# One-batch units first in a block-sparse attention and ELU feed-forward kernel: another order of loading, staging and buffering

## The chip, the cores and the metric

The kernel runs on one core of one Trainium2 chip. The metric is the device time of one execution in microseconds (us), the median of the runs. The core's engines are TensorE (PE; its weight loads are PEld), VectorE (DVE), ScalarE (ACT), GpSimd (POOL) and SyncE (SP), which issues most of the transfers.

## The reference

Attention over four batches of eight heads, 768 positions of width 64, in blocks of 32. A block of queries sees its neighbours, the first and the last block, and three sampled blocks; the first and the last block see everything. The attended rows, 3072 of width 512, then pass a feed-forward layer with an ELU. The weights arrive as 64-bit floats.

```python
scores = scale * np.matmul(q, k.transpose(0, 1, 3, 2))
mask = np.abs(blk_i - blk_j) <= window
mask = mask | (blk_i == 0) | (blk_j == 0) | (blk_i == n_blocks - 1) | (blk_j == n_blocks - 1)
for qb in range(n_blocks):
    for kb in sampled_blocks[qb]:
        mask[qb * block:(qb + 1) * block, kb * block:(kb + 1) * block] = True
attn = softmax(np.where(mask, scores, -1000000000.0))     # over the keys
x = np.matmul(attn, v)                  # rows in the order batch, position, head
h = x @ w_in                            # 3072 x 512 times 512 x 2048
g = np.where(h > 0.0, h, np.exp(np.minimum(h, 0.0)) - 1.0)
return g @ w_out                        # 3072 x 2048 times 2048 x 512
```

## The kernel before

Every operand of a matmul is held as a high and a low f16 part, and products are made of two or three such parts.

**Units.** The batches go in two pairs. A pair has 12 units of 128 query rows (four blocks of 32). `of_one` makes a unit of four blocks of one batch, `of_two` of two blocks of each batch of the pair; one special unit per pair holds the first and the last blocks. `ALONE` says how many one-batch units each batch has: 1 before, so units 0 and 1 lie in batch 0 and batch 1 alone, and from unit 2 on every unit needs the keys and values of both batches. Two units make one tile of the feed-forward layer, so there are 12 tiles; I call them tile 0 to tile 11.

**A unit** (`attention`): its queries are loaded (L640), split into high and low and turned (on PE against an identity for units below `NPE`, L385 and L680, otherwise by a transposing transfer, L377). The sampled values come into a room of `VT` by 12 band transfers or fewer (L726 to L728) and indirect gathers of GpSimd (L733); the sampled keys are copied into `kG` by GpSimd (L748, L755). Then for each of four head pairs: scores on PE (L786), their maximum on DVE (L797), the exponential on ACT (L815) into `e`, its high and low part into `p` (L299 or L297, and L820), a turn of `p` into `pT`, the product with the values on PE (L835), a sum on DVE (L844). `e` and `p` have two rooms each. At the end the rows are normalised (L852 to L854), split and turned into `xT`.

**A tile** (`ffn`): eight steps. A step has two `h` groups of 12 matmuls (L883), ACT and DVE work for the ELU (L893, L895, L891), a split into `g` (L299 or L297, and L900), and, later, two `o` groups of 6 matmuls (L906), one for each half of the tile's rows.

**Preparation.** Keys of batches 0 and 1 are loaded (L511), split (L301, L497), turned on PE and copied into `kT[0]` and `kT[1]`. Values are split and written out to a table in device memory, `vd` (L569), from which the units read them. The weights come in 32 pieces of 512 KB (L429, L433) into rooms that are free at that time (`wo_room`, later two rooms of the tag `st4`); each piece takes two passes of ACT (L439, L444), two of DVE (L451, L455), a cast and a subtraction (L462), which leave the high and the low part in `wi` and `wo`.

**What sets the order.** Each operation has a priority, the engines that may run it with a duration, and the buffers it reads and writes. `Plan.order` walks through a model of the core in time and fixes, ahead of the run, which engine runs what and in which order. On the chip each engine then goes through its list in that order; an instruction that has to wait holds back all behind it on its engine. Priorities are set at L921 to L950: the weights start at `WI`, `WID` apart; a tile at `F0 + T * U`; its units `LEAD` earlier; the second batch's keys and values at `SECOND`.

## Time and profile before

| what | value |
|---|---|
| median of 3 runs | 768.09 us (767.81 to 771.01) |
| profiled execution, first to last instruction | 780.8 us |
| PE busy | 703.2 us (90%) |
| DVE busy | 504.7 us (65%) |
| ACT busy | 406.1 us (52%) |
| POOL busy | 398.8 us (51%) |
| moved by transfers | 126.34 MB, mean 162 GB/s |
| mean granted TensorE clock | 0.934 of full speed |

A busy share is that of the whole span, so it averages a head in which the inputs and weights are prepared and a long stretch in which PE runs without a break. The profiled execution is one of its own, and 1.7% longer than the median run. Tables over stretches show which engine is full where.

### The profile page before, as it was taken

What the parts mean: (1) busy time and instruction counts of PE and PEld (TensorE: products, weight loads), DVE (VectorE), ACT (ScalarE), POOL (GpSimd) and SP (SyncE); (2) the same over time, 40 slices, a digit from 0 to 9 for tenths busy, and PEclk for the clock granted to TensorE, in tenths of its full rate; (3) what the DMA queues carried; (4) which work ended last, traced back from release to release, by engine and by line L of the source; (5) the groups of instructions that cost most, each with busy time, mean ns of one, the idle gap of its engine ahead of it and who ended that gap; (6) DMA issues with size and microseconds to landing.
All of it is one profiled execution on the core that took longest, in us unless ns stands there. A gap on an engine that the chain in (4) does not pass through costs nothing.

```text
span 780.8 us, 26302 instructions
## 1 busy us (share of the span) xinstructions
PE 703.2 (90%) x11064; PEld 476.2 (61%) x11064; DVE 504.7 (65%) x849; ACT 406.1 (52%) x723; POOL 398.8 (51%) x605
## 2 busy tenths in 40 slices
PE   6445466999999998999999999999999999999997
PEld 3334355666665765666866766657656667676663
DVE  7788778898866772767677665757555546644121
ACT  4597767897753743535575443425414344342221
POOL 2588567677553345554375454645625337443121
PEclk7555569999999999999999999999999999999999
DMA  9899998889749697769947987987349459652101
GB/s 240 263 275 288 261 257 209 215 158 208 154 91 264 187 192 164 161 133 203 221 87 142 171 149 150 183 144 166 76 94 229 69 103 216 141 97 45 38 1 27
DMA packets 217006, 126.34 MB, mean 162 GB/s; under 512 B 173944, under 2 KB 194552, under 8 KB 216888
## 3 DMA queue, kind: packets, MB, share of 16 engines
q1 hardware_dynamic: 211608, 107.09, 64.8%
q0 software_dynamic: 5280, 17.58, 8.9%
q8 instruction: 86, 1.41, 0.8%
q14 instruction: 32, 0.26, 0.1%
HBM read 82.05 MB, written 13.21 MB: 122 GB/s over the span
## 4 chain that ended last, share of the span: by engine, by line
PE 80%; issue 4%; DMA 4%; DVE 4%; ACT 3%; POOL 3%; POOLq 1%; SPq 1%; another core or an unknown queue 1%; ACTq 0%; DVEq 0%
PE o L906 32%; PE h L883 31%; PE s L786 6%; PE w L835 4%; PE av L835 2%; PE s L385 2%; DMA wo<-in_moe_w_out_dram 2%; ACT e L815 1%; PE av L385 1%; POOLq L751 1%; DMA VT<-vd 1%; POOL kG L755 1%; DMA raw<-in_sampled_blocks_dram 1%; POOL kG L748 1%
## 5 line engine op out<-in xcount | busy, mean ns | idle before, releaser
L883 PE MATMUL h<-xT,wi 128*128 128x256 f16 x2304 | 281.6, 275 | 4.7 <-DVE fe L891 4.0
L906 PE MATMUL o<-wo,g 128*128 128x512 f16 x1152 | 274.9, 381 | 0.9 <-issue 0.6
L883 PEld LDWEIGHTS <-wi 128*128 128x128 f16 x2304 | 220.0, 98 | 53.8 <-issue 7.1
L906 PEld LDWEIGHTS <-g 128*128 128x128 f16 x1152 | 107.0, 98 | 111.2 <-issue 4.2
L900 POOL TENSOR_TENSOR g<-fe,g 128x512 f16<-128x512 f32 x75 | 90.0, 1200 | 150.8 <-DVE g L299 134.8
L820 POOL TENSOR_TENSOR p<-e,p 128x512 f16<-128x512 f32 x94 | 113.1, 1206 | 93.8 <-DVE p L299 46.4
L893 ACT ACTIVATE fe<-h 128x512 f32<-128x512 f32 x96 | 57.3, 596 | 178.0 <-PE h L883 165.1
L891 DVE SCALAR_TENSOR_TENSOR fe<-h,fe 128x512 f32<-128x512 f32 x96 | 66.0, 688 | 92.9 <-ACT fe L895 84.4
L815 ACT ACTIVATE e<-s,m 128x256 f32<-128x256 f32 x208 | 86.2, 470 | 74.7 <-POOL p L820 37.1
L755 POOL COPY kG<-kT 128x128 int32 x264 | 78.5, 341 | 44.9 <-PE s L786 25.9
L797 DVE TENSOR_REDUCE m<-s 128x2 f32<-128x512 f32 x104 | 70.1, 686 | 44.4 <-PE s L786 41.4
L733 POOL DMA_INDIRECT VT<-vd,idx x66 | 64.5, 977 | 25.1 <-issue 10.1
L895 ACT ACTIVATE fe<-fe,gs 128x512 f32<-128x512 f32 x96 | 69.4, 723 | 2.4
L844 DVE TENSOR_REDUCE x<-w 128x130 f32<-128x260 f32 x64 | 27.2, 426 | 59.7 <-PE w L835 56.9
L835 PEld LDWEIGHTS <-pT 128*32 128x32 f16 x3456 | 43.2, 97 | 36.1 <-issue 33.7
L786 PE MATMUL s<-kG,qT 128*32 128x160 f16 x704 | 44.8, 247 | 9.6 <-ACT e L815 7.0
L786 PEld LDWEIGHTS <-qT 128*32 128x32 f16 x1664 | 33.2, 99 | 31.8 <-issue 26.7
L786 PE MATMUL s<-kT,qT 128*32 128x96 f16 (+1 forms) x832 | 48.5, 225 | 1.2 <-issue 1.0
L786 PE MATMUL s<-kT,qS 128*32 128x96 f16 (+1 forms) x832 | 48.3, 225 | 0.5 <-issue 0.5
L786 PE MATMUL s<-kG,qS 128*32 128x160 f16 x704 | 44.2, 246 | 4.1 <-DVE qS L299 2.7
L299 DVE CAST p<-e 128x512 f16<-128x512 f32 x59 | 32.0, 546 | 13.3 <-DMA pT<-p 6.1
L786 PEld LDWEIGHTS <-qS 128*32 128x32 f16 x1664 | 34.5, 102 | 6.0 <-DVE qS L299 3.0
(134 smaller groups left out, 812.5 us busy)
## 6 DMA issues: line engine op xcount, KB each, us to landing
VT<-vd SPq DMA_DIRECT2D x44, 195.0 KB
VT<-vd SPq DMA_DIRECT2D x22, 390.0 KB
wo<-in_moe_w_out_dram SPq DMA_DIRECT2D x12, 512.0 KB
st<-in_q_dram SPq DMA_DIRECT2D x40, 128.0 KB
out_dram<-ro SPq DMA_DIRECT2D x38, 128.0 KB
wo<-in_moe_w_in_dram SPq DMA_DIRECT2D x9, 512.0 KB
st<-in_moe_w_in_dram SPq DMA_DIRECT2D x7, 512.0 KB
VT<-vd SPq DMA_DIRECT2D x12, 260.0 KB
```

The costliest lines, as they stand in the source:

```text
L733: nc.gpsimd.indirect_dma_start(VT[0:96, 2 * vt.slot, xs[0] : xs[-1] + 1].rearrange("p b x -> p (b x)"), None, d.ap, bass.IndirectOffsetOnA ...
L755: nc.gpsimd.tensor_copy(dst[:, :, r * 16 : (r + 1) * 16], src[:, :, bass.ds(at[r], 16)])
L786: nc.tensor.matmul(dst, lhsT=qq.ap[:, h, j * BLK : (j + 1) * BLK], rhs=mv, start=first, stop=(y == 1 and qq is qS and o0 + w == 256))
L797: nc.vector.tensor_reduce(m.ap[:, 2 * c : 2 * c + 2] if sp else m.ap[:, 6:8], ss[c].ap, axis=AX.X, op=ALU.max, negate=True)
L815: nc.scalar.activation(e32.ap[:, y, :], ss[c].ap[:, y, :], AF.Exp, bias=m.ap[:, 6 + y : 7 + y])
L820: plan.add(LO, t + PITCH * hp + 1, margin=MO, fn=lambda e, e32=e32, p=p: ENG[e].tensor_tensor(p.ap[:, 1, :], flat(e32.ap), p.ap[:, 0, :], ...
L835: nc.tensor.matmul(av.ap[j * BLK : (j + 1) * BLK, y, v0:], lhsT=pts[c].ap[:, pl * 4 + y * 2 + z, j * BLK : (j + 1) * BLK], rhs=VT[:, room, ...
L883: nc.tensor.matmul(h.ap[:, a, :], lhsT=w[:, wl, cs], rhs=x.ap[:, xl, cc, :], start=(n == 0), stop=(n == 3 * NCC - 1))
L891: nc.vector.scalar_tensor_tensor(e32.ap, h.ap, -IH * GS, e32.ap, op0=ALU.mult, op1=ALU.min)
L895: plan.add({"ACT": 0.68}, p0 + 2.6, lambda e, e32=e32: nc.scalar.activation(e32.ap, e32.ap, AF.Relu, bias=gs_col, scale=-GS), r=[e32], w=[ ...
L900: plan.add(LO, p0 + 2.6, margin=MO, fn=lambda e, e32=e32, g=g: ENG[e].tensor_tensor(g.ap[:, 1], e32.ap, g.ap[:, 0], op=ALU.subtract), r=[e ...
L906: nc.tensor.matmul(o.ap, lhsT=g.ap[:, gl, f % 2, m * P : (m + 1) * P], rhs=wo[f][:, wl, :], start=(f == 0 and n == 0), stop=(f == NFC - 1 ...
```

## The change

- `ALONE` goes from 1 to 5. Units 0 to 4 now lie in batch 0 alone, units 5 to 9 in batch 1, the special unit is unit 10, and unit 11 is the one unit of two batches. The second pair of batches keeps its units.
- Only batch 0's keys and values are prepared ahead of the weights, values first. Batch 1's keys and values go through the general `keys` and `values`, at `SECOND` = 36 instead of -110; `values` can now make one batch alone.
- While `kT[1]` is empty its 12 KB per partition are three more rooms for weight pieces (`kt_room`). The first five pieces have a priority of their own, -95.
- Tiles 0 and 1 get priorities of their own: tile 0 from -50 on with 12 per step instead of 4.5, beside the weights; tile 1 from 60 on.
- `NPE` goes from 4 to 6: units 4 and 5 are turned on PE too. That adds 96 matmuls of 128x128 or 64x128 and drops 8 transposing transfers.
- From unit 6 on, except in units 9 and 10 and in the special units, odd head pairs keep `e` and `p` together in a room of the tag `st4`, which the weights and values use, in place of the tags `e` and `p`.
- The model's durations of some transfers and of the GpSimd key copies are other numbers, and so are the rules by which a weight step picks ACT or DVE (`MW`).

```diff
+class Part:
+    def __init__(self, whole, view):
+        self.whole, self.view = whole, view
+    @property
+    def ap(self):
+        return self.view()
...
-    ALONE, SPECIAL, SECOND = 1, 8, -110.0
-    MO, MC, ML, MH = -0.6, 0.0, 0.5, 0.6
+    ALONE, SPECIAL, SECOND, KT_LAST, ST_FIRST = 5, 10, 36.0, 32, 20
+    MO, MC, ML, MH, MW = -0.6, 0.0, 0.5, 0.6, 0.0
...
+    kt_room = [fixed(flat(kT[1])[:, 2048 * j : 2048 * (j + 1)].bitcast(I32).rearrange("p (e w) -> p e w", w=2))
+               for j in range(3)]
+    ROOMS = {**{j: wo_room[j] for j in range(NFC // 2)}, **{-3 - j: r for j, r in enumerate(kt_room)}}
+    used = {j: j - 20 for j in ROOMS}
...
-        free_rooms = [j for j in used if j > n // 4]
-        if n // 4 >= 4:
+        free_rooms = [j for j in used if j > n // 4 or j < -2 and n < KT_LAST]
+        if n >= ST_FIRST:
             free_rooms += [j for j in (-1, -2)]
...
-        plan.add({"SP": 0.5}, prio, load, new=[s] * tagged, w=[s] * (not tagged), dma=1.9, name=f"wl{i}")
+        plan.add({"SP": 0.5}, EARLY_AT if n < EARLY else prio, load, new=[s] * tagged, w=[s] * (not tagged), dma=1.9, name=f"wl{i}")
...
-        plan.add(SHIFT, prio, lower, margin=MH, r=[s], new=[low3], name=f"ws{i}")
+        plan.add(SHIFT, prio, lower, margin=MW, port=False, r=[s], new=[low3], name=f"ws{i}")
...
-    def values(g, c, prio):
-        n = buf("st4", [P, 2, H, VW], F16)
+    def values(g, c, prio, xs=(0, 1)):
+        n = buf("st4", [P, len(xs), H, VW], F16)
...
-                e32, p, pT = buf("e", [P, 2, 256], F32), buf("p", [P, 2, 512], F16), buf("g" if u == 1 else "pT", [P, 8, P], F16)
+                pT = buf("g" if u == 1 else "pT", [P, 8, P], F16)
+                if u >= WIDE and hp % 2 and not sp and not NUP - OFF <= u < NUP + ON:
+                    both = buf("st4", [P, 2, 512], F32)
+                    e32 = Part(both, lambda both=both: both.ap[:, 0].rearrange("p (y k) -> p y k", y=2))
+                    p = Part(both, lambda both=both: both.ap[:, 1].bitcast(F16).rearrange("p (l k) -> p l k", l=2))
+                else:
+                    e32, p = buf("e", [P, 2, 256], F32), buf("p", [P, 2, 512], F16)
...
-    EVEN, NEXT = 6, 14.0
+    EVEN, NEXT = 6, 4.0
+    WIDE, OFF, ON = 6, 3, -1
...
-    TWO, AHEAD, T, F0, LEAD, NPE = 6, 16.0, 58.0, 60.0, 130.0, 4
-    WI, WID, F2, LAG = -100.0, 3.0, 4.5, 14.0
-    V1, K1 = 70.0, 16.0
+    TWO, AHEAD, T, F0, LEAD, NPE = 6, 16.0, 58.0, 60.0, 130.0, 6
+    WI, WID, F2, LAG = -66.0, 3.0, 4.5, 14.0
+    V1, K1, SV = 70.0, 16.0, 8.0
+    EARLY, EARLY_AT = 5, -95.0
...
-    for x in range(2):
-        p = -500 if x == 0 else SECOND
-        places = [wo_place(j) for j in range(6)] if x == 0 else [wi_place(j) for j in range(2, 8)]
-        for a in range(NB // 8):
-            first_keys(x, a, places[a], p + a)
-        for a in range(NB // 8):
-            first_values(x, a, places[3 + a], p + 30 + a, room[3 * x + a])
+    F1, F2X = (-50.0, 60.0), 12.0
+    zero_rows(-485, -90)
+    room = [None, None, spare(-510, 1)[0], None, None, None]
+    for a in range(NB // 8):
+        first_values(0, a, wo_place(3 + a), -500 + a, room[a])
+    for a in range(NB // 8):
+        first_keys(0, a, wo_place(a), -490 + a)
...
+            if u == 4 * ALONE // 4:
+                for c in range(NKC):
+                    keys(0, 1, c, SECOND + 2 * c, "PE", kt_room)
+                for c in range(NKC):
+                    values(0, c, SECOND + SV + 2 * c, (1,))
...
-        ffn(U, t)
+        ffn(U, F1[U] if U < len(F1) else t, F2X if U == 0 else F2)
```

On SP's queue, at the head of the program, this stood before (`wo` and `wi` are places that the inputs use until the weights need them; `in_moe` is a weight piece):

```order
L511 DMA wo<-in_v_dram 128x8x128 x3
L511 DMA wi<-in_k_dram 128x8x128 x3
L569 DMA vd_175<-st_171 16x1040 x2
L569 DMA vd_175<-st_171 7x16x1040 x2
L429 DMA wo<-in_moe_w_in_dram 128x4x256
L640 DMA st_428<-in_q_dram 128x8x64
L429 DMA wo<-in_moe_w_in_dram 128x4x256
L569 DMA vd_175<-st_240 8x16x1040 x2
L569 DMA vd_175<-VT 7x16x1040 x2
L569 DMA vd_175<-VT 16x1040 x2
L433 DMA wo<-in_moe_w_out_dram 128x1024 x2
```

And this stands there now:

```order
L583 DMA vd_189<-st_172 8x16x1040 x2
L583 DMA vd_189<-VT 7x16x1040 x2
L583 DMA vd_189<-VT 16x1040 x2
L503 DMA vd_189<-x_178 32x1040
L655 DMA st_265<-in_q_dram 128x8x64
L444 DMA kT_71<-in_moe_w_in_dram 128x4x256 x2
L448 DMA kT_71<-in_moe_w_out_dram 128x1024
L448 DMA wo<-in_moe_w_out_dram 128x1024
L444 DMA wo<-in_moe_w_in_dram 128x4x256
L655 DMA st_431<-in_q_dram 128x8x64
```

Batch 1's keys (`wi<-in_k`) stood between batch 0's values and the first weights; now five weight pieces follow the first queries, and batch 1 is not there.

Around the first ELU step of tile 0 (`fe<-h`) DVE's list before reads as follows, with 21 of the 32 weight pieces' last DVE pass (L455) ahead of that step:

```order
L852 TENSOR_SCALAR x_2257<-x_2257 128x8
L853 RECIPROCAL x_2257<-x_2257 128x8
L854 TENSOR_TENSOR x_2257<-x_2257 128x8x64
L451 SCALAR_TENSOR_TENSOR w_2494<-wo,w_2494 128x512
L455 SCALAR_TENSOR_TENSOR wo<-wo,w_2494 128x512
L299 CAST xn_2508<-x_2257 128x512
L891 SCALAR_TENSOR_TENSOR fe_2312<-h_2164,fe_2312 128x512
```

Now it reads as follows, with 11 of the 32 (L470 is what L455 was, L919 what L891 was):

```order
L463 TENSOR_SCALAR w_1714<-kT_71 128x512
L466 SCALAR_TENSOR_TENSOR w_1714<-kT_71,w_1714 128x512
L470 SCALAR_TENSOR_TENSOR kT_71<-kT_71,w_1714 128x512
L310 CAST wo<-kT_71 128x512
L463 TENSOR_SCALAR w_1752<-kT_71 128x512
L466 SCALAR_TENSOR_TENSOR w_1752<-kT_71,w_1752 128x512
L919 SCALAR_TENSOR_TENSOR fe_1749<-h_1698,fe_1749 128x512
```

The tile has moved ahead of ten weight pieces, in among the weights.

At the end of the weights SP's queue now holds batch 1's preparation, which is not in this place before (`in_k` and `in_v` are its keys and values, `vd_510` the table its units read, `out` the rows of tile 0, half a tile each):

```order
L444 DMA kT_71<-in_moe_w_in_dram 128x4x256
L448 DMA kT_71<-in_moe_w_out_dram 128x1024 x2
L592 DMA st_3231<-in_k_dram 128x8x64
L592 DMA st_3251<-in_k_dram 128x8x64
L605 DMA st_3275<-in_v_dram 128x8x64
L592 DMA st_3307<-in_k_dram 128x8x64
L655 DMA out_dram<-ro_3305 128x512
L605 DMA st_3339<-in_v_dram 128x8x64
L614 DMA vd_510<-st_2864 32x1040
L614 DMA vd_510<-st_2864 96x1040
L655 DMA st_3422<-in_q_dram 128x8x64
L605 DMA st_3428<-in_v_dram 128x8x64
```

Five of batch 1's six value loads stand behind the first store of tile 0.

## Rows read from the trace of the kernel before

**Rows 1.** Busy time by stretch: PE, PEld, DVE, ACT, POOL, clock, transfer share, GB/s.
```profile
10.00:113.00 103.00, 52.48 (x977) 41.16 (x977) 81.41 (x124) 76.51 (x127) 65.37 (x120) 0.56 0.95 267
113.00:140.00 27.00, 19.32 (x431) 14.43 (x428) 21.47 (x36) 21.59 (x39) 17.67 (x21) 0.88 0.94 228
140.00:197.00 57.00, 55.25 (x972) 38.03 (x970) 49.90 (x79) 47.21 (x87) 42.30 (x70) 0.99 0.85 188
...
200.70:302.50 101.80, 99.64 (x1662) 66.28 (x1660) 72.33 (x122) 53.53 (x97) 45.24 (x60) 1.00 0.83 181
302.50:780.80 478.30, 465.39 (x6928) 311.28 (x6926) 269.13 (x461) 201.44 (x366) 222.79 (x312) 1.00 0.66 129
...
9.00:194.00 185.00, 124.05 (x2319) 91.14 (x2320) 151.22 (x235) 142.92 (x247) 122.77 (x207) 0.73 0.94 241
```

**Rows 2.** PE in order of time: start, us, operation, [idle before].
```profile
35.79 0.25 PE L786 MATMUL s<-kG,qS 128*32 128x160 f16 x4 [0.59 <-ACT qS L297]
...
113.00 1.97 PE L883 MATMUL h<-xT,wi 128*128 128x256 f16 x12
...
128.26 2.72 PE L883 MATMUL h<-xT,wi 128*128 128x256 f16 x12 [4.04 <-DVE fe L891]
...
199.22 1.47 PE L906 MATMUL o<-wo,g 128*128 128x512 f16 x6
...
299.69 2.76 PE L906 MATMUL o<-wo,g 128*128 128x512 f16 x12
```

**Rows 3.** SP's queue in order of time: start, us, transfer issued.
```profile
12.14 5.54 SPq L511 DMA_DIRECT2D wi<-in_k_dram  x3
...
22.31 0.47 SPq L429 DMA_DIRECT2D wo<-in_moe_w_in_dram  x1
...
45.99 0.44 SPq L511 DMA_DIRECT2D wi<-in_v_dram  x1
...
179.47 0.36 SPq L433 DMA_DIRECT2D st<-in_moe_w_out_dram  x1
```

**Rows 4.** DVE groups in 0 to 140 us: count, busy us, mean ns, idle before.
```profile
L455 DVE SCALAR_TENSOR_TENSOR wo<-wo,w 128x512 int32<-128x512 int32 x20 | 13.8, 690 | 0.7
...
L844 DVE TENSOR_REDUCE x<-av 128x130 f32<-128x260 f32 x14 | 5.9, 422 | 5.0 <-PE av L835 2.3 <-remote 2.1 <-PE s L385 0.6
...
L497 DVE SCALAR_TENSOR_TENSOR n<-st,n 128x512 f16<-128x512 f32 x6 | 5.0, 848 | 0.1
...
L299 DVE CAST wi<-wo 128x512 f16<-128x512 f32 x3 | 1.4, 453 | 0.1
```

**Rows 5.** DVE in order of time: the last weight piece's last pass on DVE.
```profile
192.89 0.70 DVE L455 SCALAR_TENSOR_TENSOR st<-st,w 128x512 int32<-128x512 int32 x1
```

**Rows 6.** Transfers in 0 to 140 us, all queues together.
```profile
DMA packets 36747, 35.67 MB, mean 255 GB/s; under 512 B 10488, under 2 KB 29560, under 8 KB 36728
```

**Rows 7.** Chain of waits, merged pieces: start, us, what.
```profile
142.90 0.46 PE s L385 x8
...
189.29 1.01 PE s L786 x64
190.30 5.35 PE h L883 x48
195.64 0.46 PE av L835 x32
...
197.52 1.29 PE o L906 x6
```

**Rows 8.** SP's queue: the first and last of 12 band transfers into VT.
```profile
80.53 0.50 SPq L726 DMA_DIRECT2D VT<-vd  x1
...
86.71 0.30 SPq L728 DMA_DIRECT2D VT<-vd  x1
```

**Rows 9.** SP's queue: a piece of the second pair's values, loaded and stored.
```profile
213.17 0.40 SPq L590 DMA_DIRECT2D st<-in_v_dram  x1
...
233.55 0.79 SPq L599 DMA_DIRECT2D vd<-st  x2
```

More of the change, by code (lines that the diff above doesn't have):

```diff
@@ L377, in turn16 @@
             plan.add({"SP": 1.3}, t, lambda e: nc.sync.dma_start_transpose(dst(), flat(src.ap)),
-                     r=[src], new=new, w=w, dma=2.4, name=name)
+                     r=[getattr(src, "whole", src)], new=new, w=w, dma=1.5, land=0.9, name=name)
             return
+        got = getattr(src, "whole", src)
         pt = buf(bank, [P, 8, P], F16, ps)
@@ L385, in go @@
                 nc.tensor.transpose(pt.ap[:, i, :], f[:, i * P : (i + 1) * P], ident16)
-        plan.add({"PE": 0.46}, t, go, r=[src], new=[pt], code=16, name=name + "p")
+        plan.add({"PE": 0.46}, t, go, r=[got], new=[pt], code=16, name=name + "p")
         def leave(e):
@@ L478, with zero_rows, put @@
     vd += [[(buf("vd1", [ROWS, 2 * RW], F16, dr), (0, 1))] for _ in range(1, NPAIR)]
-    def zero_rows(prio):
-        z = buf("st4", [P, 2 * RW], F16)
+    def zero_rows(prio, later):
+        z = buf("x32", [P, RW], F16)
         plan.add({"POOL": 0.6}, prio, lambda e: nc.gpsimd.memset(z.ap[0:BLK, :], 0.0), new=[z], name="zero")
         for g in range(NPAIR):
-            for n in (0, NB - 1):
-                for d, xs in vd[g]:
-                    def put(e, d=d, xs=xs, n=n):
-                        nc.sync.dma_start(d.ap[n * BLK : (n + 1) * BLK, :], z.ap[0:BLK, 0 : RW * len(xs)])
-                    plan.add({"SP": 0.45}, prio, put, r=[z], new=[d] if n == 0 else [],
-                             w=[d] if n else [], dma=0.3, name=f"z{g}")
+            for d, xs in vd[g]:
+                for n in (0, NB - 1):
+                    for i in range(len(xs)):
+                        def put(e, d=d, n=n, i=i):
+                            nc.sync.dma_start(
+                                d.ap[n * BLK : (n + 1) * BLK, i * RW : (i + 1) * RW], z.ap[0:BLK, :])
+                        first = n == 0 and i == 0
+                        plan.add({"SP": 0.45}, prio if xs == (0,) else later, put, r=[z], new=[d] if first else [],
+                                 w=[] if first else [d], dma=0.3, name=f"z{g}")
     def split(prio, s, n, high, low, scale, new, name="", src=None):
@@ L574, in first_values, with keys @@
                          name=f"vs0{x}.{a}")
-    def keys(g, x, c, prio, via="DMA"):
+    def keys(g, x, c, prio, via="DMA", over=()):
         s, n = buf("st2", [P, H, D], F32), buf("n2", [P, H, 2, D], F16)
@@ L654, in next_kslot @@
         return (kslot_n[0] - 1) % rooms["kG"]
+    kept = []
     def attention(u, t, via):
@@ L728, in load @@
                         nc.sync.dma_start(room[BLK:P, 1], d.ap[(i - 1) * BLK : (i + 2) * BLK, :])
-                plan.add({"SP": 0.6 * len(parts)}, t - 8, load, r=[d for d, _ in there], new=[vt], dma=1.8, name=f"vt{u}")
+                plan.add({"SP": 0.6 * len(parts)}, t - 8, load, r=[d for d, _ in there], new=[vt], dma=1.5, land=2.0, name=f"vt{u}")
                 def gather(e, vt=vt, parts=parts):
@@ L735, in gather, with fresh @@
                             bass.IndirectOffsetOnAxis(ap=idx[0:96, i : i + 1], axis=0))
-                plan.add({"POOL": 1.0 * len(parts)}, t - 8, gather, r=[d for d, _ in there], w=[vt], dma=1.7, land=5.0, port=False, name=f"vg{u}")
+                plan.add({"POOL": 1.0 * len(parts)}, t - 8, gather, r=[d for d, _ in there], w=[vt], dma=1.5, land=3.7, port=False, name=f"vg{u}")
+                def fresh():
+                    kept.append((g, bx))
+                    return kept[-1 - rooms["kG"] : -rooms["kG"]] != [(g, bx)]
                 def copy(e, kg=kg, y=y):
@@ L756, in copy @@
                                 dst[:, :, r * 16 : (r + 1) * 16], src[:, :, bass.ds(at[r], 16)])
-                plan.add({"POOL": 1.75 if two else 2.5}, t - 6, copy, r=keys_in, new=[kg], name=f"kg{u}")
+                plan.add({"POOL": (1.5 if two else 2.1) + (1.1 if fresh() else 0.0)}, t - 6, copy, r=keys_in, new=[kg], name=f"kg{u}")
         x32 = buf("x32", [P, H, D + 1], F32)
```

30 lines of the change are left out of this document (13 added, 17 removed).

## The prediction

> **What bounds the kernel now.** I read the busy time by stretch first [rows 1]. From 140 us on PE works without a break (55.25 of 57 us, then 99.64 of 101.8, then 465.39 of 478.3) at a clock of 0.99 to 1.00. Ahead of that, from 10 to 113 us, it is busy for 52.48 of 103 us at a mean clock of 0.56, which is nearly the lower of its two levels (1.2 and 2.4 GHz), while DVE is busy for 81.41, ACT for 76.51, and the transfer engines for 0.95 of the time. So the kernel has two parts: a head that feeds PE too little, and a body that PE bounds. What is done for PE's work in the body changes nothing; the time is won or lost by how soon PE has its work.
>
> Next PE's own list in order of time [rows 2]. The first scores run at 35 us, the first `h` group only at 113 us, tile 0's last `o` group ends at 200.7 us (199.22 + 1.47) and tile 2's at 302.5 us (299.69 + 2.76). SP's queue shows why the head is slow [rows 3]: batch 1's keys are issued at 12.14 us, ahead of the first weight piece at 22.31; its values up to 46 us, in among the weights; and the last weight piece only at 179.47. PE ran full from 140 us all the same, since it had attention and tile 1 to fill with.
>
> **What the change moves.** Batch 1's keys and values (6 blocks of 512 KB, 12 splits on each of two engines, the value tables) leave the head and come behind the weights. Tile 0 comes in among the weights. So I ask when tile 0 ends now, call that X, and add PE's remaining list.
>
> **Step 1, the work up to the last weight piece.** DVE is the busiest helper to that point (151.22 us between 9 and 194, ACT 142.92, POOL 122.77) [rows 1], so I count its list. Up to the last pass of the last weight piece it held 170 instructions of the 0.69 us kind (the row of the weight pass, 690 ns), 22 casts of 0.45, 22 sums of 0.42 and 9 low parts of queries of 0.85 [rows 4]: 117.3 + 10.0 + 9.3 + 7.6 = 144.2 us, without the shortest instructions. It now holds 137, 29, 16 and 5: 94.5 + 13.1 + 6.8 + 4.2 = 118.6 us. The 25.6 us less are batch 1's splits and copies, and units 4 and 5 with part of tile 1, which came ahead of the last piece and now come behind it.
>
> **Step 2, how fast DVE gets through.** Before, DVE began at 9 us and ended that pass at 193.6 (192.89 + 0.70) [rows 5]: 144.2 / 184.6 = 0.78 of the time. At that rate the new list ends at 9 + 118.6 / 0.78 = 161 us. In its fullest long stretch, 140 to 197 us, DVE was busy for 0.875 [rows 1]; times the share that my count has of the measured busy time (144.2 / 151.2) that is 0.835, and the list ends at 151 us. I expect a rate nearer to the better one, since transfers press less. Up to 140 us 35.67 MB were moved [rows 6]. Up to the last weight piece there now stand 38 blocks of 512 KB (19.9 MB), queries, value table, bands, gathers and batch 1's first keys (my sum over SP's and POOL's lists: 13.3 MB), together 33.2 MB, which at the 267 GB/s of the busiest stretch [rows 1] take 124 us. So transfers end ahead of DVE. I take 154 us. Before, tile 0 ended 7.1 us behind DVE's last pass (200.7 against 193.6); I take 6. **X = 160 us**, with 144 (DVE at 0.91, half way from 0.835 to full, and 5 us behind) and 177 (the old rate, and 16 us lost to waits that I can't see) as ends.
>
> **Step 3, PE's list behind X.** From tile 0's last group to tile 2's the list before holds 25 `h` groups, 32 `o`, 18 products with values, 20 scores and 10 turns. From the chain a group of `h` takes 5.35 / 4 = 1.34 us, `o` 1.29, a product 0.46, a score 1.01 / 2 = 0.505, a turn 0.46 [rows 7]: 33.5 + 41.3 + 8.3 + 10.1 + 4.6 = 97.8 us by count, 101.8 in the trace. The new list holds 30, 32, 24, 27 and 24 (a double turn counted as two): 40.2 + 41.3 + 11.0 + 13.6 + 11.0 = 117.1, and by the same ratio 121.9 us. Behind tile 2 the `h` and `o` groups are the same 144 and 144; 5 scores, 2 products and 2 turns come on top, 2.5 + 0.9 + 0.9 = 4.3, by the ratio 4.5 us on 478.3. So the new span is X + 121.9 + 478.3 + 4.5 = X + 604.7, and 764.7 us for X = 160: **16.1 us less than 780.8**. X = 176 would be no change.
>
> **The smaller parts.** The 96 matmuls that turn units 4 and 5 on PE are in the counts. More rooms for `e` and `p` from unit 6 on I cost at nothing: PE idles only 12.9 us behind 302.5 and 2.2 us between 200.7 and 302.5 [rows 1]; they can bring back 5 us at most, and cost as much if values wait for a room. One-batch units make GpSimd read positions twice per key copy; POOL was busy for 122.77 of 185 us and its list up to that point is shorter too, so I cost it at nothing, and at 5 us if POOL is full.
>
> The profiled execution is 12.7 us longer than the median of 768.09; I carry the difference over as it is: 768.1 - 16.1 = **752 us**. About 0.5% (3.8 us) is what a measurement of this kernel can tell from no change.
>
> **Rivals.**
>
> *Batch 1 comes late.* Unit 5 needs its values. Five of its six value loads stand on SP's queue behind the store of tile 0's first half, which waits for tile 0, and behind the last of them come the table's stores and 12 band transfers (80.53 to 87.0, 6.5 us [rows 8]). PE reaches that unit's first product 46 us behind X (14 `h`, 11 `o`, 5 products, 8 scores, 15 turns: 18.8 + 14.2 + 2.3 + 4.0 + 6.9 = 46.2). DVE has 34 instructions of some 0.65 us between its last weight pass and the last value split, 22 us; with the bands that is 28.5, some 17 us ahead of need, out of which the landings come. Against that: in the second pair it took 20.4 us from a value load's issue to that of its store (213.17 to 233.55 [rows 9]). Six pieces in two rooms at that pace are 61 us, with the bands 68, and 22 us late: 752 + 22 = 774 us, slower. It decides from 16 us of lateness on. Half that lateness gives 763 us, about no change.
>
> *The clock stays low.* From 10 to 113 us PE ran at 0.56, and one `h` group behind an idle time of 4.04 us took 2.72 us [rows 2] where a group at full clock takes 1.34. Tile 0's groups now come weight by weight, with idle time between them. From the first `h` to X PE has 18 `h`, 16 `o`, 8 scores, 8 products and 19 turns, 24.1 + 20.6 + 4.0 + 3.7 + 8.7 = 61.1 us at full clock. DVE's list up to the last product of unit 1 is 46 us, so the first `h` is due at 9 + 46 / 0.78 = 68 us. At half clock the 61.1 us become 122, and X = 190 us if PE never waits: 782 us, slower. It decides where the clock averages below 61.1 / 108 = 0.57. Against it: from 113 to 140 us, with `h` groups and waits mixed, the clock was 0.88 at 19.32 of 27 us busy [rows 1]. The Trainium skill's page "TensorE: Matmul & The Clock Gate", section "HAM oscillation — how this bites in real kernels", tells of such kernels: short bursts of matmuls with transfer waits between them fall back to the low clock in every wait. By that rule this rival would be the forecast; the row of 0.88 speaks against it, the single group behind 4.04 us for it.
>
> *The helpers run full.* With three more rooms for waiting weights, DVE could run at its count's full rate: 9 + 118.6 = 128 us, just behind the transfers' 126; X = 134, and 726 us.
>
> *The gain is given back.* If PE's early idle time only moves (four units of attention now lie beside tile 2, where two lay before), ACT and DVE are fuller there: DVE's count is 53 us for PE's 63. A tenth of the 122 us lost to waits is 12 us: 764 us, no change.
>
> **How the numbers follow.** Forecast 752 us, chance 0.66, its own range 738 to 764. Batch 1 late 0.14 (0.04 of it still faster, 0.05 no change, 0.05 slower). Low clock 0.05. Full helpers 0.09. Given back 0.06. Faster by over 0.5%: 0.66 + 0.09 + 0.04 = 0.79; within 0.5%: 0.05 + 0.06 + 0.01 of the low clock = 0.12; slower: 0.05 + 0.04 = 0.09. The range is 737 to 768: it takes in X from 144 to 176 and leaves out the far half of the full helpers and what is slower.
>
> **What would show it.** Right: first scores near 25 us, since DVE's list up to their maximum is 16 us behind 9; first `h` at 60 to 75 us; last weight piece issued at 125 to 145; tile 0 ended at 150 to 168; tile 2 near 282; PE full from X on. Wrong: tile 0's end behind 176 us, a clock below 0.6 between 70 and 150 us, or a hole on PE ahead of the sixth unit's products with the band transfers into `VT` as its end. If tile 2 ends at 282 us and the whole is still no shorter, the body has new stalls and step 3 is the wrong one.

## The result, and the profile after

The changed kernel takes 779.18 us (778.4 to 782.07) beside 768.65 us for the kernel before: a ratio of 1.0132, interval 1.0102 to 1.0161. It is 1.3% slower, where I had named 752 us and faster. Its profiled execution has a span of 776.4 us, and 778.4 us in all. Ratios and intervals, here and below, are of the runs in a chip's usual state, without one slower run each of e12 and e13, and are not quite the quotients of the medians beside them.

The kernel before, profiled again on another chip (e1 below), has a span of 768.2 us and not 780.8, and takes 770.62 us. That is the base to compare with; in what follows "before" in a table is e1, and "rows" are the rows ahead of the prediction.

The head did what the change says. Busy time by stretch of the changed kernel, with the columns of [rows 1]:

```profile
10.00:113.00 103.00, 68.09 (x1108) 50.81 (x1110) 77.65 (x132) 72.00 (x119) 60.71 (x102) 0.67 0.90 253
113.00:140.00 27.00, 18.67 (x312) 12.50 (x311) 23.47 (x39) 22.31 (x38) 18.33 (x22) 0.94 0.69 192
140.00:165.00 25.00, 18.25 (x264) 13.27 (x264) 18.75 (x31) 16.28 (x27) 12.94 (x19) 0.80 0.17 44
165.00:197.00 32.00, 32.00 (x562) 23.77 (x561) 21.62 (x35) 27.21 (x46) 18.76 (x46) 1.00 0.58 152
197.00:230.00 33.00, 28.84 (x449) 17.48 (x448) 19.98 (x35) 17.08 (x30) 19.37 (x29) 0.95 1.02 218
230.00:300.00 70.00, 67.09 (x1394) 46.21 (x1394) 55.97 (x93) 45.43 (x84) 44.19 (x81) 1.00 0.83 170
```

And of the kernel before (e1):

```profile
10.00:113.00 103.00, 54.71 (x985) 43.54 (x986) 85.23 (x126) 77.72 (x129) 65.27 (x121) 0.56 0.95 265
113.00:140.00 27.00, 19.30 (x423) 13.80 (x421) 22.63 (x34) 21.61 (x39) 18.36 (x26) 0.82 0.95 236
140.00:197.00 57.00, 56.17 (x1011) 39.20 (x1010) 50.46 (x81) 48.10 (x89) 40.64 (x68) 0.99 0.86 188
197.00:300.00 103.00, 102.44 (x1714) 68.63 (x1713) 73.38 (x125) 54.77 (x100) 48.25 (x66) 1.00 0.84 182
```

The reader is to see two things. PE is busy 13.4 us longer up to 113 us, at a clock of 0.67 instead of 0.56. And from 140 us on it is no longer full where it was before: 50.25 of 57 us from 140 to 197 us against 56.17, and 28.84 of 33 us from 197 to 230, at a transfer share of 1.02.

PE in order of time, as in [rows 2], changed kernel: the first scores, the first `h` groups, a wait for the last weight pieces, the end of tile 0, the hole in tile 1 with its neighbours, the end of tile 2.

```profile
32.22 0.32 PE L807 MATMUL s<-kG,qT 128*32 128x160 f16 x3 [2.05 <-ACT qT L308]
...
80.71 3.59 PE L911 MATMUL h<-xT,wi 128*128 128x256 f16 x16
...
146.74 2.31 PE L911 MATMUL h<-xT,wi 128*128 128x256 f16 x10 [3.71 <-POOL wi L477]
...
164.33 2.75 PE L934 MATMUL o<-wo,g 128*128 128x512 f16 x12
...
217.45 1.47 PE L934 MATMUL o<-wo,g 128*128 128x512 f16 x6
222.91 0.53 PE L863 MATMUL av<-VT,pT 128*32 128x130 f16 x32 [3.99 <-DVE x L872]
223.82 2.29 PE L934 MATMUL o<-wo,g 128*128 128x512 f16 x6
...
294.35 2.76 PE L934 MATMUL o<-wo,g 128*128 128x512 f16 x12
```

The same two ends before (e1):

```profile
196.71 1.47 PE L906 MATMUL o<-wo,g 128*128 128x512 f16 x6
...
295.09 2.76 PE L906 MATMUL o<-wo,g 128*128 128x512 f16 x12
```

Tile 0 ends at 167.1 us (164.33 + 2.75), against 198.2 before; tile 2 at 297.1, against 297.9. So 31 us of lead at tile 0 are 0.7 us at tile 2, and at the end it is behind by 8.2. The table takes the work out: the lead in time, and the same with the difference in PE's list up to that tile added or taken away (matmul groups by the durations of [rows 7], times 1.02). A falling second row is time lost, not work done earlier or later.

| end of tile | 0 | 1 | 2 | 3 | 4 | 5 | 6 | 7 | 9 | 11 |
|---|---|---|---|---|---|---|---|---|---|---|
| lead of the changed kernel, us | 31.1 | 12.6 | 0.7 | 2.7 | 2.2 | -5.0 | -7.9 | -8.8 | -12.4 | -7.7 |
| the same, net of PE's work | 12.5 | 7.5 | 1.9 | 4.6 | 2.4 | 1.6 | -1.4 | -2.7 | -3.0 | -2.1 |

Of the 31.1 us, 18.6 are work put off; 12.5 are won. 5.0 of them are lost in tile 1, 5.6 in tile 2, 4.0 behind it, and 5.6 us are the turns that PE has on top at the end.

**Tile 1.** The hole of 3.99 us above is put down to a sum of DVE (`x`, L872), which is short. What DVE was held by, changed kernel, DVE in order of time:

```profile
202.25 0.73 DVE L515 SCALAR_TENSOR_TENSOR n<-st,n 128x512 f16<-128x512 f32 x1
...
211.49 0.86 DVE L688 COPY qS<-qT 64x1024 f16<-64x1024 f16 x2 [1.91 <-DMA qT<-n]
...
216.31 0.42 DVE L872 TENSOR_REDUCE x<-av 128x130 f32<-128x260 f32 x1
222.10 0.42 DVE L688 COPY qS<-qT 64x1024 f16<-64x1024 f16 x1 [5.37 <-DMA qT<-n]
222.44 0.42 DVE L872 TENSOR_REDUCE x<-av 128x130 f32<-128x260 f32 x1
```

DVE waits 5.37 us for the turned queries of unit 7, and the sum that PE needs stands behind that copy. By the order of the list these queries had been split at 202.98 us (the first row). Why they are late stands on SP's queue, changed kernel:

```profile
193.65 0.82 SPq L614 DMA_DIRECT2D vd<-st  x2
...
195.01 0.89 SPq L743 DMA_DIRECT2D VT<-vd  x1
...
202.97 0.42 SPq L745 DMA_DIRECT2D VT<-vd  x1
203.56 1.35 SPq L388 DMA_TRANSPOSE qT<-n  x1
...
209.07 0.50 SPq L743 DMA_DIRECT2D VT<-vd  x1
211.49 0.30 SPq L744 DMA_DIRECT2D VT<-vd  x1
...
215.45 0.30 SPq L745 DMA_DIRECT2D VT<-vd  x1
215.90 1.26 SPq L388 DMA_TRANSPOSE qT<-n  x1
217.21 5.17 SPq L655 DMA_DIRECT2D st<-in_q_dram  x5
```

The last store of batch 1's values is issued at 193.65 us; the 12 bands of unit 5 follow, the turn of unit 6's queries, the 12 bands of unit 6, then, at 215.90, the transposing transfer of unit 7's queries, with the transfer engines at a share of 1.02. DVE's copy starts 6.2 us after its issue. SP's queue is held up on the way: eight transfers go out from 203.56 us on, and the ninth only at 211.49, when the first of them, the turn of unit 6's queries, has landed (DVE's copy of it starts at 211.49). That is 7.9 us from its issue, where the planner counts 3.7. Behind the hole PE's clock is low for a while: it is 0.67 from 223 to 227 us, and the group of six `o` takes 2.29 us where it took 1.47.

**Behind 300 us** PE's waits were for exponentials in the kernel before. PE's waits in 300 to 780 us (line, what was waited for, us in total, times, longest), changed kernel:

```profile
PE w L863 <- DMA pT<-p: 2.4, 3, 1.1
PE av L863 <- DMA pT<-p: 2.0, 4, 0.7
PE w L863 <- DMA pT<-st: 1.7, 1, 1.7
```

and before (e1):

```profile
PE s L786 <- ACT e L815: 1.6, 3, 0.9
PE w L786 <- ACT e L815: 1.2, 1, 1.2
```

6.1 us of waits for transposing transfers of `p` are new. One of them, changed kernel, SP's issue and PE's product:

```profile
550.90 1.28 SPq L388 DMA_TRANSPOSE pT<-p  x1
...
555.98 0.53 PE L863 MATMUL w<-VT,pT 128*32 128x130 f16 x32 [1.11 <-DMA pT<-p]
```

It is 5.1 us from issue to product; for the turns issued at 430.64, 483.57 and 498.36 us it was 4.6, 6.2 and 6.6. The planner now counts 1.3 + 1.5 + 0.9 = 3.7 us for it; the old number gave 1.3 + 2.4 + 2.5 = 6.2.

### The profile page after: what moved, and what is told of

It is laid out like the page before. It is cut to its first block, busy times and chain, and to the rows that moved or that the text cites. A ratio compares the mean times of both kernels' runs of the same rounds, so it can differ in the third digit from the quotient of the medians.

```text
span 776.4 us, 26639 instructions
## 1 busy us (share of the span) xinstructions
PE 703.0 (91%) x11160; PEld 478.6 (62%) x11160; DVE 492.2 (63%) x844; ACT 427.0 (55%) x744; POOL 389.4 (50%) x605
## 4 chain that ended last, share of the span: by engine, by line
PE 36%; DMA 6%; DVE 5%; issue 3%; POOL 2%; ACT 1%; POOLq 1%; SPq 0%; DVEq 0%; ACTq 0%
PE o L934 17%; PE h L911 15%; DMA pT<-p 4%; PE s L807 2%; PE w L863 2%; DMA st<-in_k_dram 1%; DVE m L818 1%; DMA pT<-st 1%; DVE fe L919 1%; POOLq L772 1%; ACT e L843 0%; POOL kG L776 0%; DVE x L872 0%; PE av L863 0%; POOL p L848 0%
## 5 line engine op out<-in xcount | busy, mean ns | idle before, releaser
L919 DVE SCALAR_TENSOR_TENSOR fe<-h,fe 128x512 f32<-128x512 f32 x96 | 65.9, 687 | 102.1 <-ACT fe L923 100.2
L776 POOL COPY kG<-kT 128x128 int32 x264 | 82.5, 353 | 38.1 <-issue 20.9
L848 POOL TENSOR_TENSOR p<-e,p 128x512 f16<-128x512 f32 x55 | 66.1, 1205 | 67.2 <-DVE p L310 34.2
L843 ACT ACTIVATE e<-s,m 128x256 f32<-128x256 f32 x148 | 61.5, 471 | 55.5 <-DVE m L818 44.8
L872 DVE TENSOR_REDUCE x<-w 128x130 f32<-128x260 f32 x64 | 27.1, 424 | 35.7 <-PE w L863 34.7
L515 DVE SCALAR_TENSOR_TENSOR n<-st,n 128x512 f16<-128x512 f32 x42 | 35.9, 864 | 11.2 <-ACT n L308 10.9
L308 ACT ACTIVATE n<-st 128x512 f16<-128x512 f32 x35 | 21.7, 625 | 32.8 <-DMA st<-in_q_dram 14.5
```

Of the source, the lines that this page charges most:

```text
L776: nc.gpsimd.tensor_copy(dst[:, :, r * 16 : (r + 1) * 16], src[:, :, bass.ds(at[r], 16)])
L843: nc.scalar.activation(e32.ap[:, y, :], ss[c].ap[:, y, :], AF.Exp, bias=m.ap[:, 6 + y : 7 + y])
L848: plan.add(LO, t + PITCH * hp + 1, margin=MO, fn=lambda e, e32=e32, p=p: ENG[e].tensor_tensor(p.ap[:, 1, :], flat(e32.ap), p.ap[:, 0, :], ...
L919: nc.vector.scalar_tensor_tensor(e32.ap, h.ap, -IH * GS, e32.ap, op0=ALU.mult, op1=ALU.min)
```

## The experiments

No kernel leaves out any part of the computation. Chips differ, so every ratio is to the kernel before on the same chip: it took 770.6 us on the chip of e1 to e4, 782.4 to 784.9 on that of e5 to e12, 784.5 on that of e13 to e16 and 785.2 on that of e17 and e18. Net leads of e5 to e18 are taken against the trace with 780.8 us, which is of the slower kind.

### Is 780.8 us the kernel before?

**e1**, the kernel before, unchanged.

> The kernel before, unchanged, for a second profile. Theory A: the profiled execution that the prediction was worked on (span 780.8 us) was an unusually long one; then this profile has a span of 764 to 770 us, and tile 0 and tile 2 end 8 to 15 us earlier than 200.7 and 302.5 us. Rival B: this kernel always runs some 13 us longer under the profiler; then the span is 778 to 784 us again, with a timed median of 768 to 769.

Measured: 770.62 us, ratio 1.000 (0.998 to 1.002), span 768.2, as theory A had it; but tiles 0 and 2 end only 2.5 and 4.6 us earlier, not 8 to 15. The two traces of one program part in the body: tile 3 takes 60.9 us here and 68.2 in the first trace. PE of the first trace at that place:

```profile
310.81 0.61 PE L385 MATMUL av<-ident,p 128*128 128x128 f16 x8 [3.29 <-issue]
...
341.37 0.23 PE L786 MATMUL s<-kT,qS 128*32 128x96 f16 x2 [0.49 <-issue]
342.13 0.26 PE L786 MATMUL s<-kG,qT 128*32 128x160 f16 x2 [0.47 <-issue]
342.89 0.21 PE L786 MATMUL s<-kT,qT 128*32 128x96 f16 x1 [0.49 <-issue]
```

In e1 PE idles once from 300 to 345 us, 0.94 us for an exponential. "issue" is idle time in which PE waited for nothing that the profile shows. So a part of the 12.7 us that I carried over sits in the terms of my sum.

**e9** and **e17**, the changed kernel, unchanged, on two more chips.

> The changed kernel, unchanged, beside the next three on the same chip. Expected: 1.010 to 1.017 of before again. If the loss depends on the chip it is nearer to the 1.025 of the runs of its variants on the slower chip.

> The changed kernel unchanged, to stand on the same chip beside e18. On a chip on which TensorE shows no idle time that the profile can't name (as in the first comparison): ratio to before 1.010 to 1.016, and the hole of some 4 us in tile 1, ended by VectorE behind the turned queries of unit 7. On a chip that shows such idle time: 1.014 to 1.021, and some 8 us of it between 165 and 300 us.

Measured: e9 799.16 us, 1.017 (1.014 to 1.0201); e17 801.61 us, 1.0187 (1.014 to 1.0235). The result holds on these chips too. On these two the hole of 3.99 us isn't there; tile 0 ends 7 to 8 us later (174.1 and 175.1 us), and PE idles as in the first trace of before. e9, PE in order of time:

```profile
233.42 0.27 PE L807 MATMUL s<-kG,qS 128*32 128x160 f16 x4 [0.20 <-issue]
234.18 0.24 PE L807 MATMUL s<-kT,qS 128*32 128x96 f16 x3 [0.49 <-issue]
234.92 0.21 PE L807 MATMUL s<-kT,qS 128*32 128x96 f16 x1 [0.50 <-issue]
...
235.67 0.23 PE L807 MATMUL s<-kG,qT 128*32 128x160 f16 x1 [0.47 <-issue]
```

and e17, PE's largest wait from 165 to 300 us:

```profile
PE s L807 <- issue: 8.6, 14, 1.2
```

About half a microsecond at a time, some 0.75 us apart, in scores and other short matmuls. From 165 to 300 us that is 8.0 us in e9 and 8.6 in e17, 1.2 in the first trace of before, none in the changed kernel's first trace; from 165 us to the end it is 10.3, 11.0, 6.4 and 0.2. So the changed order, with its scores and turns packed into tiles 1 and 2, pays more for it on chips that have it. What it is stays open.

### What the changed place of batch 1 is worth

**e3** puts batch 1 back: layout of units, place and weights' rooms.

```diff
-    ALONE, SPECIAL, SECOND, KT_LAST, ST_FIRST = 5, 10, 36.0, 32, 20
+    ALONE, SPECIAL, SECOND, KT_LAST, ST_FIRST = 1, 8, -110.0, 0, 16
```

> The changed kernel with units cut as before (one one-batch unit per batch), batch 1's keys and values ahead of the weights (priority -110) and none of the three extra rooms for weights; the priorities of tiles 0 and 1, the turns on PE, the joint rooms and the model's durations stay as changed. Theory that the units and batch 1's place are what costs: 765 to 771 us, like before. Rival that they are the gain and the rest costs more than it shows: 783 to 800 us.

Measured: 805.01 us, 1.0429 (1.0377 to 1.0481), beyond even the rival's range. Tile 0 ends 26 us later than in the changed kernel, and the body loses more: PE waits 13.6 us for transposing transfers behind 300 us, with batch 1 in its old place. Among the change's other parts, then, the new place and layout of batch 1 are no loss but a gain, of some 3%.

**e11** puts batch 1 ahead of the weights and leaves the layout of units.

```diff
-    ALONE, SPECIAL, SECOND, KT_LAST, ST_FIRST = 5, 10, 36.0, 32, 20
+    ALONE, SPECIAL, SECOND, KT_LAST, ST_FIRST = 5, 10, -110.0, 0, 20
```

> The changed kernel with batch 1's keys and values ahead of most weights (priority -110) and without the three extra rooms, units and all else as changed. Theory: tile 0 ends 15 to 25 us later than in the changed kernel (182 to 192 us), since DVE's 12 splits and 6 copies of batch 1 come ahead, but unit 5 finds its values, so tile 2 ends at 290 to 300 us and the time is 1.005 to 1.015 of before. Rival: what holds tile 2 is not batch 1, and it ends 15 us later too, 1.03.

Measured: 809.07 us, 1.0328 (1.0274 to 1.0381), against 1.017 of e9 on the same chip; the rival had named 1.03. Tile 0 ends at 204.0 us, 29.9 later than in e9, and tile 2 at 317.3, 1.9 later. The net lead goes from -8.3 to -13.7 us in tiles 1 and 2, in e9 from 8.0 to -11.7: that loss is smaller by 14.3 us, in the theory's direction, but the head has lost 16.3.

**e10** has only batch 1's values earlier, amid the weights.

```diff
-    V1, K1, SV = 70.0, 16.0, 8.0
+    V1, K1, SV = 70.0, 16.0, -60.0
```

> The changed kernel with batch 1's values (not its keys) 68 earlier in priority (SV = -60), so that they are loaded, split and stored in among the weights. Theory: tile 2 waits for unit 5, which waits for batch 1's value table; in the changed kernel and in the run without the turns of units 4 and 5 tile 2's first h stood at 230 us, whether tile 1 ended at 229 or at 211. With the values early the first h of tile 2 comes at 205 to 218 us, tile 2 ends at 284 to 292, and the time falls by 6 to 13 us to 0.995 to 1.005 of before. Rival: the keys' rooms or the weights themselves set it, and tile 2 starts at 228 us or later again, 1.010 to 1.02.

Measured: 799.72 us, 1.0201 (1.0158 to 1.0244); the profiled run was a shorter one, span 792.2. Tile 0 ends at 181.8 us, 7.7 later than in e9, and tile 2 at 306.6, 8.8 earlier: the loss in tiles 1 and 2 is down to 4.1 us (net lead 1.2, 0.8, -2.9) from 19.7, and the lead it would have eaten is gone too. Of these 15.6 us less, 6.1 are idle time that the profile can't name (1.9 us from 165 to 300 us, in e9 8.0). The rest speaks for the rival "batch 1 comes late" as what eats the lead, and says that bringing it earlier costs as much in the head.

### The smaller parts

**e2**: no shared rooms for `e` and `p`.

```diff
-    WIDE, OFF, ON = 6, 3, -1
+    WIDE, OFF, ON = 99, 3, -1
```

> The changed kernel with the joint room for e and p switched off in all units (WIDE = 99), so that e and p have their own two rooms each as before. Theory: the rooms matter little, 776 to 783 us (1.01 to 1.018 of before). Rival: odd head pairs wait for a room that the values of the second pair hold, or the turned p of that room comes late, and this is the loss; then 765 to 772 us.

Measured: 796.55 us, 1.0322 (1.0273 to 1.0372). Up to tile 4 the net lead is that of the changed kernel within 3.5 us; tiles 5 and 6 lose 18 us. PE's largest wait in 300 to 780 us:

```profile
PE w L863 <- DMA pT<-p: 12.4, 8, 4.2
```

With the second line for such transfers (1.2 us) it is 13.6 us, where the changed kernel has 6.1.

**e16**: the kernel before with the shared rooms alone.

```diff
-                e32, p, pT = buf("e", [P, 2, 256], F32), buf("p", [P, 2, 512], F16), buf("g" if u == 1 else "pT", [P, 8, P], F16)
+                if u >= WIDE and hp % 2 and not sp and not NUP - OFF <= u < NUP + ON:
+                    both = buf("st4", [P, 2, 512], F32)
...
+    WIDE, OFF, ON = 6, 3, -1
```

> The kernel before with one part of the change alone: e and p of odd head pairs share a room of the weights' store from unit 6 on; planner's numbers and all else as before. The kernel before has no TensorE waits for turned p behind 300 us, so rooms have nothing to hide there: theory, 0.997 to 1.005. Rival (the rooms are worth time by themselves, as 17 us in the changed order): 0.98 to 0.99.

Measured: 788.62 us, 1.0044 (1.0024 to 1.0064). Without late turns of `p` (PE waits for none behind 300 us) the rooms are worth nothing, and cost a little.

**e6**: the kernel before with the new duration of transposing transfers alone.

```diff
-                     r=[src], new=new, w=w, dma=2.4, name=name)
+                     r=[src], new=new, w=w, dma=1.5, land=0.9, name=name)
```

> The kernel before with the changed kernel's durations of a transposing transfer (1.5 and 0.9) and nothing else. Theory: it gets the same waits, PE for pT by 5 to 15 us, and 776 to 786 us. Rival: the numbers do no harm in another order, 767 to 773 us.

Measured: 798.89 us, 1.0202 (1.017 to 1.0235); the profiled run was a shorter one, span 787.8. PE's largest waits in 300 to 780 us:

```profile
PE w L835 <- DMA pT<-p: 4.4, 4, 1.7
PE w L835 <- issue: 4.0, 2, 2.0
```

The waits for turned `p`, which the kernel before doesn't have, come with this number. Nothing else of the change is in e6, and it is 2% slower. That the waits are what it loses by isn't shown: in the profiled run the net lead is -8.1 us at tile 0, -6.8 at tile 2 and -7.2 at the end, so against the trace of 780.8 us all of its loss lies in the head, ahead of these waits. The other four runs, 798.57 to 800.08 us, weren't traced.

**e5** and **e8**: the changed kernel with the old number, and the same without shared rooms.

```diff
-                     r=[getattr(src, "whole", src)], new=new, w=w, dma=1.5, land=0.9, name=name)
+                     r=[getattr(src, "whole", src)], new=new, w=w, dma=2.4, name=name)
```

> The changed kernel with one pair of numbers set back: the model's durations of a transposing transfer (2.4 us of the transfer engines and 2.5 us to land, in place of 1.5 and 0.9). Theory: the changed kernel's order gives such a transfer 3.7 us from its issue where the trace shows 4.6 to 6.2, so PE and DVE reach their instructions before the data; with the old numbers PE's waits for pT and DVE's for qT go, 760 to 769 us. Rival: the units and the place of batch 1 are the loss, 775 to 783 us.

> The changed kernel with the old durations of a transposing transfer and without the joint rooms for e and p. Theory: the joint rooms were worth 17 us only because they let p be turned earlier and so hid late transfers; then it is within 5 us of the run with the old durations alone. Rival: the rooms are worth the same here, 12 to 20 us over that run.

Measured: e5 802.11 us, 1.025 (1.0189 to 1.0311); e8 803.1 us, 1.0282 (1.0219 to 1.0346). PE waits for turned `p` are gone in e5 and 1.1 us in e8, and the rooms are worth 0.3% instead of nearly 2%, which fits that they cover late turns; but the 2% come from the chip of e2 and the 0.3% from one of the slower kind. The kernel is no faster than e9's 1.017. e5's net lead is 15.6 at tile 0, 13.5 at tile 1 and -2.0 at tile 2: this order loses little in tile 1 and 15.5 us in tile 2, with 14.4 us of PE idle from 165 to 300 us (6.9 of it "issue").

**e14**: the planner told of a later landing, nearer to the trace.

```diff
-                     r=[getattr(src, "whole", src)], new=new, w=w, dma=1.5, land=0.9, name=name)
+                     r=[getattr(src, "whole", src)], new=new, w=w, dma=1.5, land=2.2, name=name)
```

> The changed kernel, its planner told that a transposing transfer lands 2.2 us behind its 1.5 (0.9 in the changed kernel; the trace has 4.6 to 6.2 us from issue to the first product that uses it, the planner 3.7). Theory (late turns of p cost the body some 6 us by waits): waits of TensorE for transposing transfers behind 300 us fall from 6.1 us to under 2, and the ratio to before falls to 1.005 to 1.013. Rival (any other order of this list has waits of its own, as setting the old 2.4 us back had): the waits on turns go and others come, the ratio stays at 1.013 to 1.025.

Measured: 809.88 us, 1.0306 (1.0269 to 1.0343). The waits fell as expected, from 6.1 us (5.0 in e9) to 1.6, and the time rose, beyond the rival's range too: tile 2 ends at 324.2 us, with a hole of 3.39 us on PE that ends with ACT's copy into `xT` and a clock of 0.83 from 230 to 300 us. So taking the late turns away is not enough: the order changes everywhere, and this one has waits of its own, as the rival said.

**e7**: old durations for bands, gathers and copies of keys.

```diff
-                plan.add({"SP": 0.6 * len(parts)}, t - 8, load, r=[d for d, _ in there], new=[vt], dma=1.5, land=2.0, name=f"vt{u}")
+                plan.add({"SP": 0.6 * len(parts)}, t - 8, load, r=[d for d, _ in there], new=[vt], dma=1.8, name=f"vt{u}")
...
-                plan.add({"POOL": (1.5 if two else 2.1) + (1.1 if fresh() else 0.0)}, t - 6, copy, r=keys_in, new=[kg], name=f"kg{u}")
+                plan.add({"POOL": 1.75 if two else 2.5}, t - 6, copy, r=keys_in, new=[kg], name=f"kg{u}")
```

> The changed kernel with the model's durations of the band transfers, the gathers and the GpSimd key copies set back, those of the transposing transfers left as changed. Theory: these numbers are not the cause, 774 to 786 us with PE's waits for pT still there. Rival: the gathers land later than the new numbers say, and setting them back gives 764 to 771 us.

Measured: 802.53 us, 1.0262 (1.0218 to 1.0307). Setting these numbers back doesn't mend the loss; it costs 0.9% more than e9.

### Units turned on PE

**e4** has four such units, as before, **e12** the same with e10's early values.

```diff
-    TWO, AHEAD, T, F0, LEAD, NPE = 6, 16.0, 58.0, 60.0, 130.0, 6
+    TWO, AHEAD, T, F0, LEAD, NPE = 6, 16.0, 58.0, 60.0, 130.0, 4
```

> The changed kernel with units 4 and 5 turned by transposing transfers again (NPE = 4). 96 matmuls fewer, 5.4 us of PE at full clock. Theory that PE bounds all behind tile 0: 772 to 776 us, some 5 us less than the changed kernel. Rival that the transfers would come late in the busy stretch behind the weights: 779 us or more.

> Values early, and units 4 and 5 turned by transfers again (96 matmuls fewer). Theory: with tile 2 no longer held by the value table PE's work counts in full, so it is 3 to 6 us faster than values early alone, 0.988 to 1.0 of before. Rival: the transposing transfers of units 4 and 5 come late in the weights and it is no faster.

Measured: e4 780.69 us, 1.0134 (1.0082 to 1.0186), as the changed kernel; e12 809.17 us, 1.023 (1.0174 to 1.0286), no faster than e10, as its rival had it. e12's net lead is -1.9, -4.9 and -15.6 us: with the values early tiles 1 and 2 lose 13.7 us all the same, so e10's small loss there doesn't carry over to this order. e4 is the clearest case of a lead that isn't kept: tile 0 ends at 156.8 us and tile 1 at 210.8, 10 and 18 us ahead of the changed kernel, and tile 2 at 295.1. Net lead: 17.2, 17.5, -1.6. Its 5.5 us of saved turns are gone as well.

**e13** and **e18** go the other way: units 6 and 7 turned on PE too, which takes unit 7's transposing transfer out of tile 1.

```diff
-    TWO, AHEAD, T, F0, LEAD, NPE = 6, 16.0, 58.0, 60.0, 130.0, 6
+    TWO, AHEAD, T, F0, LEAD, NPE = 6, 16.0, 58.0, 60.0, 130.0, 8
```

> The changed kernel with one number more: units 6 and 7 (of 48), too, have their queries and scores turned by TensorE and not by transposing transfers. Theory (a transposing transfer stuck behind fresh band transfers makes the hole in tile 1): VectorE no longer waits for unit 7's turned queries, the hole of 3.99 us ahead of unit 5's last product is gone or under 1.5 us, and tile 2 ends 2 to 4 us earlier; the turns bring some 5 us of new TensorE work, so the ratio to before is 1.010 to 1.020, about the changed kernel's own. Rival (batch 1 is simply late, its bands and not the queries end the wait): the hole stays at 3 us or more, and the ratio rises by the new turns to 1.020 to 1.026.

> Units 6 and 7, too, turned by TensorE, beside e17 on one chip. Theory (the transposing transfer behind the fresh bands makes the hole): no hole over 1.5 us ended by VectorE in tile 1, and tile 2 ends 1 to 4 us before that of e17. If the turns cost more than the hole: tile 2's end later than in e17 by up to 3 us and the whole later by 2 to 8. Rival (batch 1 late): the hole stays, at 3 us or more.

Measured: e13 810.13 us, 1.034 (1.0292 to 1.0388); e18 807.53 us, 1.0307 (1.0275 to 1.034), beside 1.0187 of e17 on the same chip. Neither has a hole in tile 1 that DVE ends, but e17 and e9 have none either, so the cause of the 3.99 us as read from the first trace (a transposing transfer behind 24 fresh bands) wasn't put to the test. The hole does stand in the traces of e2 and, there in tile 2, of e4, whose chip is of the kind of the changed kernel's first trace; PE in e2, then in e4:

```profile
221.07 0.85 PE L863 MATMUL av<-VT,pT 128*32 128x130 f16 x32 [3.70 <-DVE x L872]
...
215.41 0.84 PE L863 MATMUL av<-VT,pT 128*32 128x130 f16 x32 [4.18 <-DVE x L872]
```

In both DVE has just waited for turned queries, 5.68 and 8.51 us, with bands ahead of them on SP's queue (24 in e2, 12 in e4). Tile 2 ended 3.9 us earlier in e18 than in e17, as the theory said, with more work in it; the whole was 5.9 us later by the medians, lost from tile 3 on.

**e15**: e13 and e14 together.

> Both edits: units 6 and 7 turned by TensorE, and 2.2 us for the landing of a transposing transfer. If the hole in tile 1 and the waits for turns are what the changed kernel loses by, the ratio to before is 1.000 to 1.010 with 5 us of new turns in it; if each order has its own waits, 1.013 or more.

Measured: 808.17 us, 1.0284 (1.0258 to 1.031). In this order the waits for turned `p` behind 300 us are back at 6.2 us, though the planner counts the later landing; tile 2 ends at 314.0 us, and tiles 4 and 5 lose another 15.1 us of net lead. None of the kernels beats the kernel before.

## Why the prediction was wrong

By its own sum, put on e1's base: tile 0's end to tile 2's end is 99.7 us there for 97.8 by count, so the new list is 117.1 x 99.7 / 97.8 = 119.4; behind tile 2 it is 470.3 + 4.5 = 474.8; the span is X + 594.2, and the time 2.0 more. X = 160 gives 756.2 us. The measured 778.4 us of the profiled execution are then

756.2 + 7.1 (X) + 10.6 (tiles 1 and 2) + 4.5 (behind them) = 778.4.

- **The difference carried over.** I took the profiled execution's 12.7 us as a constant beside the sum. It was mostly stalls inside my terms (X + 604.7 against X + 594.2). The two errors nearly cancel: 752 instead of 756.2. The wrong step cost 4.2 us.
- **Step 1, the count.** The count of the list held, and so did the sum over transfers: 33.2 MB forecast by the last weight piece,

```profile
DMA packets 30926, 33.19 MB, mean 237 GB/s; under 512 B 10060, under 2 KB 24524, under 8 KB 30908
```

  in 0 to 140 us of the changed kernel. The last piece was issued at 135.4 to 138.4 us (125 to 145 named).
- **Step 2, X.** DVE's last weight pass ended at 158.6 us, where I took 154, and tile 0 8.5 us behind it, where I took 6: X = 167.1, inside the bounds of 144 and 177. DVE went through its list at 118.6 / 149.6 = 0.79, the old rate of 0.78 and not the better one of 0.835. That transfers press less did not help: from 140 to 165 us they are at 0.17, DVE at 18.75 of 25 us, and PE, which DVE's copies wait for, waits itself 3.71 us for a weight. First scores (32.2 instead of 25 us) and first `h` (80.7 instead of 60 to 75) were late from the start.
- **Step 3, the list behind X.** This is the step that failed. The 19.7 us of added list were right as a count: the trace holds the same 30, 32, 24, 27 and 24 groups between the ends of tiles 0 and 2. "PE full from X on" was not. Tiles 1 and 2 take 130.0 us and not 119.4, and tile 2 ends at 297.1 us where I named 282. PE idles 7.0 us from 165 to 300 us (before: 0.4), most of it in one wait; changed kernel, then before (e1):

```profile
PE av L863 <- DVE x L872: 4.0, 1, 4.0
...
PE o L906 <- issue: 0.4, 1, 0.4
```

  PE's clock of 0.95 over 33 us (197 to 230) is an estimated 1.7 us; the other 2.3 us I can't assign. Behind tile 2 it is 479.3 us and not 474.8, with 6.1 us of waits for transposing transfers.
- **What I left out.** I costed the shared rooms at nothing and the planner's new durations not at all. e6 shows that one duration alone makes the kernel before 2.0% slower; e2 shows that without the rooms the changed kernel waits 13.6 us for turned `p` instead of 6.1 and takes 1.9% more by the ratios. A change in a planner's duration is a change of the order everywhere, and PE's list of before, which hardly idled behind 140 us, was no warrant for the new one.
- **The rivals.** "Batch 1 comes late" named the place: a hole ahead of the sixth unit's product, with the bands around it. It was 4 us and not 22, and by way of the transposing transfer behind the bands: the last table store came at 193.65 us, 26.6 us behind X, where the need was put 46 us behind X. "The gain is given back" named 12 us for tiles 1 and 2 and was nearest to the 10.6; it lacked the body. "The clock stays low" didn't come: 0.94 from 113 to 140 us and 0.91 from 140 to 197. The Trainium skill's page "TensorE: Matmul & The Clock Gate", section "HAM oscillation — how this bites in real kernels", says that bursts with transfer waits between fall back to the low clock. The trace agrees for a single wait (2.29 us for 1.47 behind 3.99 us of idle time, the clock at 0.67); from 113 to 140 us, with 8.33 us of idle time in 27, it doesn't: there the clock is 0.94. "The helpers run full" is out by the rate of 0.79 (its "126" should read 124, as in step 2).

What is shown: the lead exists, net of work 12.5 us; all or most of it is lost in tiles 1 and 2 in every order in which batch 1 comes behind the weights (changed kernel, e2, e4, e5, e7, e8, e9, e13, e14, e15, e17, e18), and moving batch 1 forward gives the lead up in the head (e10, e11, e12) and makes that loss much smaller in e10 and e11, but not in e12. e6 shows the cost of one duration, not the way it comes about. What stays open: none of the parts that were set back one by one (rooms, turns on PE, two groups of durations, batch 1 with its units) brings the kernel to the time before, and others never were set back alone (among them the priorities of tiles 0 and 1, the delay `NEXT` of tile 0's second unit, the rule `MW` and the three extra rooms), so which of them make the loss isn't known; the hole was read from three traces (the changed kernel's first, e2 and e4), and no run took it away on a chip that has it; and which resource tiles 1 and 2 lack isn't settled (transfers are at 1.02 from 197 to 230 us, but in e4 and e5 tile 1 goes well and tile 2 is lost).
